# A key-value product in two parts, read in another column order, with half of its fold right behind it

## The chip, the core and the metric

The kernel runs on one core of a Trainium2 chip. A core has a matrix engine (TensorE, "PE" in the profile; its weight loads are listed apart as "PEld"), a vector engine (VectorE, DVE), a scalar engine for activation functions and copies (ScalarE, ACT), a general engine (GpSimd, POOL) and a queue engine that issues most transfers (SyncE, SP). TensorE writes its products to PSUM, an accumulation memory; VectorE and ScalarE read them from there. The main on-chip memory is SBUF, with 128 partitions.

The metric is the device time of one execution in microseconds. The kernel before took 261.73 us (median of three runs, 260.96 to 261.99).

## The reference: two blocks and a gate

x has 2048 tokens of width 640. Block A is linear attention with 32 heads of 20 features; block B is a mixer with an MLP; a gate per token mixes them.

```python
qkv = x @ wqkv                       # q, k, v: 32 heads of 20
phi = lambda t: where(t > 0, t + 1, exp(t)) + 1e-6
pq, pk = phi(q), phi(k)
kv = einsum("bhsd,bhse->bhde", pk, v)          # one 20 x 20 block per head
z = einsum("bhsd->bhd", pk)
o = einsum("bhqd,bhde->bhqe", pq, kv) / (einsum("bhqd,bhd->bhq", pq, z)[..., None] + 1e-6)
a = o @ wo

h = gelu(layernorm(x) @ w1)          # then four quarters of h shifted by +1, -1, +2, -2 tokens
x1 = x + shifted(h) @ w2
b = x1 + gelu(layernorm(x1) @ w3) @ w4          # w3: 640 x 1728
out = g * a + (1 - g) * b            # g = sigmoid((x * gate_w).sum(-1))
```

## The kernel before, in words

The work is written out in a fixed order: each engine runs its instructions in the order of the program text, and semaphores hold an instruction until its inputs and buffers are ready. Tokens are cut into 16 chunks of 128 (four tiles of 512); widths of 640 into 5 chunks of 128.

Block A is rearranged so that v is never computed. First pk = phi(x wk) is made for all tokens (L191 and after), then pq = phi(x wq), transposed (q_unit, L242). `g_unit` (L340) forms G = pk^T x, 640 by 640 and summed over all tokens, along with z. It takes the 640 features of pk in five sets j, each of every fifth feature, so that set j holds features m*5 + j for m = 0 to 127. Each set is copied by ScalarE and turned by a transposing transfer into `gT[:, :, j * 128 : (j + 1) * 128]`. So gT, for each of the 5 chunks of x's width, has 640 columns, ordered by set j and then by m; four consecutive m belong to one head (4 times 5 is 20 features).

The kv product (`kv_unit`, L423) multiplies gT with wv, head by head in effect: groups of 3 heads (60 columns), two of them side by side on two halves of the array, six such group pairs (`NG = 6`; the last has a single group of 2 heads and 40 columns). For each it accumulates over 5 chunks: 55 matmuls. wv is the stationary operand, with 64 or 40 columns; gT is streamed. The result holds all cross products of three heads; a mask (`bmask`) keeps the blocks in which both heads agree. VectorE applies it while it copies from PSUM into `kvT` (L428 for five groups, L432 for the last).

The fold multiplies kvT with wo, `m_mm` (L441), so that attention becomes pq M with M = kv wo; ScalarE evicts each fold group (`m_evac`, L447), M goes through memory outside the core (`m_store`, L450, `m_load`), and the attention products use it much later (L539). The denominator needs u = sum of z times pq, in float32 (`den_add`, L261, on VectorE; u lies over part of xT). It is split into two bfloat16 parts so that TensorE can sum it exactly enough: `den_hi` casts u in two halves of the tokens on ScalarE (L264), `den_lo` takes the difference on VectorE (L267), and `den_mm` sums both over the features of a head (L272).

Block B runs around it. `w1_unit` (L395) multiplies the normalised tokens by w1 for one tile of 512 tokens and column blocks of 128; ScalarE evicts with GELU into hsT at shifted places (L402). Column block 4 holds the rest of the four quarters; its GELU goes into `hx` (L405) and VectorE copies four strips of it to shifted places (L408). Then w2 (L508), layer norm, w3 (L558), attention (L539), w4 (L597, L633) follow, tile by tile.

Every product takes its PSUM buffer from `pair()`, which hands out four buffers of two banks in turn. A product therefore waits until the product four calls earlier has been evicted. At the place of the change the order of calls before is: w1 of tile 0 in three units, the two casts of u, kv, den_lo, layer norm of two chunks of the last tile, w1 of tile 1 for column blocks 0, 1 and 4, the fold of groups 0 to 2, w1 of tile 1 for blocks 2 and 3, the fold of groups 3 to 5 and the denominator.

Of the kernel before, what the change touches and what calls it, by code (L numbers as in the profile page):

```python
# [8 lines left out]
ALU = mybir.AluOpType  # L9
BF16 = mybir.dt.bfloat16  # L10
F32 = mybir.dt.float32
# [5 lines left out]
def kernel(  # L17
# [13 lines left out]
    nc = tc.nc  # L31
    P = 128
    S, D = A_x.shape[1], A_x.shape[2]
    F = B_w3.shape[1]
    H, Dh = 32, 20
    NCH = S // P
    TS = 512
    NT = S // TS
    CPT = TS // P
    DC = D // P  # L40
# [5 lines left out]
    shifts = [1, -1, 2, -2]  # L46
    YMAX = 60.0
    GH = 3
    GW = GH * Dh
    NG = 6  # L50
    HP = P // 2
# [7 lines left out]
    const = ctx.enter_context(tc.tile_pool(name="const", bufs=1))  # L59
# [8 lines left out]
    def pair():  # L68
        return ps.tile([P, 2, 512], F32, name="pp")
# [3 lines left out]
    hsT = const.tile([P, DC, S + 4], BF16)  # L73
# [7 lines left out]
    kvT = const.tile([P, NG, HP], BF16)  # L81
# [10 lines left out]
    hmask = const.tile([P, H], F32)  # L92
    z = const.tile([P, DC], F32)
    hm_bf = const.tile([P, H], BF16)
    bmask2 = const.tile([P, 2, GH * 4], F32)
    bmask = const.tile([P, GH * 4], F32)
    ylog = const.tile([P, NCH], F32)
    gate = const.tile([P, NCH], F32)
    omg = const.tile([P, NCH], F32)
# [12 lines left out]
    gT = wk_sb  # L112
# [35 lines left out]
    for g in (0, 2):  # L148
# [8 lines left out]
                            base=0, pattern=[[-1, P]], channel_multiplier=1)  # L157
    for c in range(0, NCH, CPT):
# [3 lines left out]
                            base=0, pattern=[[-4, H]], channel_multiplier=1)  # L162
    nc.gpsimd.affine_select(out=hmask[:], in_=hmask[:], compare_op=ALU.is_ge, fill=0.0,
                            base=3, pattern=[[4, H]], channel_multiplier=-1)
    nc.gpsimd.tensor_copy(hm_bf[:], hmask[:])
    nc.gpsimd.memset(bmask2[:], 1.0)
    nc.gpsimd.affine_select(out=bmask2[:], in_=bmask2[:], compare_op=ALU.is_ge, fill=0.0,
                            base=0, pattern=[[-HP, 2], [-Dh, GH], [0, 4]], channel_multiplier=1)
    nc.gpsimd.affine_select(out=bmask2[:], in_=bmask2[:], compare_op=ALU.is_ge, fill=0.0,
                            base=Dh - 1, pattern=[[HP, 2], [Dh, GH], [0, 4]], channel_multiplier=-1)  # L170
    nc.gpsimd.tensor_tensor(bmask[:], bmask2[:, 0, :], bmask2[:, 1, :], op=ALU.add)
    nc.gpsimd.memset(kvT[:], 0.0)
    for dc in range(DC):
# [58 lines left out]
    for c in range(2, NCH):  # L232
        pt = pair()
# [19 lines left out]
    halves = (slice(0, S // 2), slice(S // 2, S))  # L253
# [9 lines left out]
    def den_hi(sl):  # L263
        nc.scalar.copy(xT[:, 4, sl], u[:, sl])  # L264
# [57 lines left out]
    def ln1_apply(c, eng=nc.vector):  # L322
        t, cc = divmod(c, CPT)
        if cc == 0:
            lnxT[t] = lnx_p.tile([P, DC, TS], BF16, name="lnxT")
        lnx = work.tile([P, D], BF16, name="ln")
        if eng is nc.scalar:
            nc.scalar.activation(lnx[:], x_sb[:, c, 0:D], ACT.Identity, bias=nmr1[:, c:c + 1], scale=rstd1[:, c:c + 1])
        else:
            nc.vector.tensor_scalar(lnx[:], x_sb[:, c, 0:D], mv1[:, c, 0:1], rstd1[:, c:c + 1],  # L330
                                    op0=ALU.subtract, op1=ALU.mult)
        nc.sync.dma_start_transpose(lnxT[t][:, :, cc * P:(cc + 1) * P], lnx[:])
# [57 lines left out]
    def w1_mm(t, fcs):  # L390
        pt = pair()
        for i, fc in enumerate(fcs):
            for dc in range(DC):
                w = w1_sb[:, dc, CG * fc:CG * fc + P] if fc < 4 else w1x[:, dc, :]
                nc.tensor.matmul(pt[:, i, :], lhsT=w, rhs=lnxT[t][:, dc, :], start=(dc == 0), stop=(dc == DC - 1))  # L395
        return pt

    def w1_evac(t, fcs, pt):
        for i, fc in enumerate(fcs):
            if fc < 4:  # L400
                o = 2 + shifts[fc] + t * TS
                nc.scalar.activation(hsT[:, fc, o:o + TS], pt[:, i, :], ACT.Gelu_apprx_tanh)  # L402
            else:
                hx = hx_p.tile([P, TS], BF16, name="hx")
                nc.scalar.activation(hx[:], pt[:, i, :], ACT.Gelu_apprx_tanh)  # L405
                for g in range(4):
                    o = 2 + shifts[g] + t * TS
                    nc.vector.tensor_copy(hsT[32 * g:32 * (g + 1), 4, o:o + TS], hx[32 * g:32 * (g + 1), :])  # L408

    def w1_unit(t, fcs):  # L410
        w1_evac(t, fcs, w1_mm(t, fcs))

    w1_split = ((0, 1), (2, 3), (4,))

    def kv_unit():
        pt = pair()
        for g in range(NG):
            for fc in range(DC):
                for v in range(2 if g < NG - 1 else 1):
                    q = 2 * g + v  # L420
                    h0, h1 = GH * q, min(GH * (q + 1), H)
                    c1 = min(GW * q + HP, D)
                    nc.tensor.matmul(pt[HP * v:HP * v + c1 - GW * q, 0, g * GW:g * GW + (h1 - h0) * Dh],  # L423
                                     lhsT=wv_sb[:, fc, GW * q:c1],
                                     rhs=gT[:, fc, 0:D].rearrange("p (j h i) -> p j h i", j=DC, h=H)[:, :, h0:h1, :],
                                     start=(fc == 0), stop=(fc == DC - 1))
        n = NG - 1
        nc.vector.tensor_tensor(  # L428
            kvT[:, 0:n, 0:GW].rearrange("p g (r j) -> p g j r", j=DC),
            pt[:, 0, 0:n * GW].rearrange("p (g j r) -> p g j r", g=n, j=DC),  # L430
            bmask[:].unsqueeze(1).unsqueeze(1).broadcast_to([P, n, DC, 4 * GH]), op=ALU.mult)
        nc.vector.tensor_tensor(  # L432
            kvT[0:2 * Dh, n, 0:2 * Dh].rearrange("p (r j) -> p j r", j=DC),
            pt[0:2 * Dh, 0, n * GW:n * GW + 2 * Dh].rearrange("p (j r) -> p j r", j=DC),
            bmask[0:2 * Dh, 0:8].unsqueeze(1).broadcast_to([2 * Dh, DC, 8]), op=ALU.mult)

    def m_mm(g, pt, b0=0):
        for v in range(2 if g < NG - 1 else 1):
            k = GW if g < NG - 1 else 2 * Dh
            for hf in range(2):  # L440
                nc.tensor.matmul(pt[HP * hf:HP * (hf + 1), b0 + v, 0:HD], lhsT=kvT[HP * v:HP * v + k, g, :],  # L441
                                 rhs=wo_sb[HP * v:HP * v + k, g, hf * HD:(hf + 1) * HD], start=True, stop=True)

    def m_evac(g, pt, b0=0):
        n = 2 if g < NG - 1 else 1
        dst = mst4[:, g] if g < 4 else mst2[:, g - 4]
        nc.scalar.copy(dst[:, 0:n, :], pt[:, b0:b0 + n, 0:HD])  # L447
# [6 lines left out]
    def m_load():  # L454
        nc.sync.dma_start(m_sb[:], m_dram[0:D, :].rearrange("(r j) e -> r j e", j=DC))

    for fcs in w1_split:
        w1_unit(0, fcs)
    for sl in halves:
        den_hi(sl)  # L460
    kv_unit()
    for sl in halves:
        den_lo(sl)
    for cc in range(2, CPT):
# [1 line left out]
    ln1_rstd(3, 2, CPT)  # L466
    for cc in range(2):
        ln1_apply(3 * CPT + cc)
    for fc in (0, 1, 4):
        w1_unit(1, (fc,))  # L470
    mps = [pair() for _ in range(3)]
    for g in range(3):
        m_mm(g, mps[g])
    for g in range(3):
        m_evac(g, mps[g])
    for fc in (2, 3):
        w1_unit(1, (fc,))
    mps += [pair() for _ in range(2)]
    for g in range(3, 5):
# [256 lines left out]
```

## Time and profile before

| what | value |
|---|---|
| median of three runs | 261.73 us |
| the profiled execution | 261.98 us, span 260.3 us |
| TensorE busy | 253.8 us, 98% of the span |
| VectorE, ScalarE, GpSimd busy | 147.7, 108.0, 32.4 us |
| kv matmuls (L423) | 55, from 76.86 us |
| fold matmuls (L441) | 12 from 81.23 us, 10 from 84.23 us |
| mask into kvT (L428, L432) | 1030 ns and 356 ns on VectorE |
| casts of u (L264) | two, 1.98 us together, on ScalarE |
| granted TensorE clock | 0.999 of full speed |

The span runs from the first to the last instruction; the execution's time is 1.7 us more. In rows of the profile the first numbers are counts, busy time and the mean duration of one instruction in ns, or, in timelines, the start from the span's beginning and the length. Matmuls overlap in a pipeline, so the mean duration of one is longer than the distance from one to the next.

### The profile page before, as it was taken

What the parts mean: (1) busy time and instruction counts of PE and PEld (TensorE: products, weight loads), DVE (VectorE), ACT (ScalarE), POOL (GpSimd) and SP (SyncE); (2) the same over time, 40 slices, a digit from 0 to 9 for tenths busy, and PEclk for the clock granted to TensorE, in tenths of its full rate; (3) what the DMA queues carried; (4) which work ended last, traced back from release to release, by engine and by line L of the source; (5) the groups of instructions that cost most, each with busy time, mean ns of one, the idle gap of its engine ahead of it and who ended that gap; (6) DMA issues with size and microseconds to landing.
All of it is one profiled execution on the core that took longest, in us unless ns stands there. A gap on an engine that the chain in (4) does not pass through costs nothing.

```text
span 260.3 us, 4189 instructions
## 1 busy us (share of the span) xinstructions
PE 253.8 (98%) x1625; PEld 149.6 (57%) x1648; DVE 147.7 (57%) x272; ACT 108.0 (42%) x168; POOL 32.4 (12%) x86
## 2 busy tenths in 40 slices
PE   6999999999999999999999999999999999999995
PEld 3677555688854644565464566455565546465543
DVE  2488778799999988498300398600287610125132
ACT  3455444465788546432343323342322344342100
POOL 4000040023410340032000131000022000000000
PEclk9999999999999999999999999999999999999999
DMA  8999999016672797964022124213123412211011
GB/s 186 193 139 329 368 272 336 36 29 125 123 103 55 102 154 198 270 199 94 4 40 40 20 53 96 76 24 60 20 52 72 101 23 40 42 48 54 22 51 52
DMA packets 57358, 27.98 MB, mean 108 GB/s; under 512 B 45394, under 2 KB 56442, under 8 KB 57338
## 3 DMA queue, kind: packets, MB, share of 16 engines
q1 hardware_dynamic: 56896, 27.22, 44.8%
q10 hardware_dynamic: 442, 0.49, 0.6%
q8 instruction: 13, 0.21, 0.4%
q14 instruction: 7, 0.06, 0.1%
HBM read 12.86 MB, written 3.47 MB: 63 GB/s over the span
## 4 chain that ended last, share of the span: by engine, by line
PE 96%; DMA 2%; issue 1%; SPq 0%; ACT 0%; DVE 0%
PE pp L558 21%; PE pp L597 16%; PE pp L508 8%; PE pp L340 8%; PE pp L539 8%; PE pp L395 8%; PE pp L242 8%; PE pp L191 8%; PE pp L633 5%; DMA wk_sb<-in_A_wqkv_dram 2%; PE pp L568 1%; PE pp L589 1%; PE pp L423 0%; SPq L122 0%; PE pp L649 0%
## 5 line engine op out<-in xcount | busy, mean ns | idle before, releaser
L558 PE MATMUL pp<-lnxT,w_sb 128*128 128x512 bf16 x249 | 59.8, 379 | 0.6
L560 ACT ACTIVATE h<-pp 128x1024 bf16<-128x1024 f32 (+1 forms) x28 | 27.0, 963 | 56.1 <-PE pp L558 56.1
L597 PE MATMUL pp<-h,w_sb 128*128 128x512 bf16 (+1 forms) x228 | 42.4, 343 | 0.3
L558 PEld LDWEIGHTS <-w_sb 128*128 128x128 bf16 x260 | 25.0, 98 | 27.0 <-issue 0.3
L511 DVE TENSOR_TENSOR x<-pp,x_sb 128x640 f32<-128x640 f32 x16 | 13.1, 816 | 40.1 <-PE pp L508 40.0
L597 PEld LDWEIGHTS <-w_sb 128*128 128x128 bf16 x234 | 22.6, 98 | 19.6 <-issue 1.0
L183 ACT ACTIVATE e<-pp 128x640 bf16<-128x640 f32 (+1 forms) x26 | 21.5, 828 | 9.5 <-PE pp L242 9.4
L303 POOL TENSOR_SCALAR rstd<-mv 128x1 f32<-128x1 f32 (+2 forms) x22 | 9.1, 416 | 127.9 <-DVE mv L309 126.9
L539 PE MATMUL pp<-m_sb,pqT 128*128 128x320 bf16 x160 | 24.3, 299 | 0.0
L545 DVE SCALAR_TENSOR_TENSOR x<-pp,gate,x 128x640 f32<-128x640 f32 x16 | 14.1, 883 | 17.9 <-PE pp L539 12.6
L508 PE MATMUL pp<-w_sb,hsT 128*128 128x320 bf16 x160 | 23.9, 300 | 0.0
L191 PE MATMUL pp<-wk_sb,xT 128*128 128x320 bf16 (+1 forms) x160 | 22.1, 300 | 1.2 <-DMA wk_sb<-in_A_wqkv_dram 1.2
L340 PE MATMUL pp<-x_sb,pk 128*128 128x320 bf16 (+1 forms) x160 | 22.0, 300 | 0.0
L242 PE MATMUL pp<-xT,hsT 128*128 128x512 bf16 x98 | 21.6, 379 | 0.1
L340 PEld LDWEIGHTS <-pk 128*128 128x128 bf16 x160 | 18.8, 117 | 3.2
L508 PEld LDWEIGHTS <-hsT 128*128 128x128 bf16 x160 | 15.5, 98 | 8.4 <-issue 0.4
L610 DVE SCALAR_TENSOR_TENSOR oc<-pqT,omg,x 128x640 bf16<-128x640 bf16 x12 | 10.5, 877 | 17.0 <-DMA pqT<-hx 17.0
L539 PEld LDWEIGHTS <-pqT 128*128 128x128 bf16 x160 | 15.6, 98 | 7.7
L191 PEld LDWEIGHTS <-xT 128*128 128x128 bf16 x160 | 15.6, 98 | 7.5 <-issue 1.4
L395 PE MATMUL pp<-lnxT,w_sb 128*128 128x512 bf16 x77 | 17.9, 379 | 0.3 <-ACT hx L405 0.2
L242 PEld LDWEIGHTS <-hsT 128*128 128x128 bf16 x100 | 11.7, 117 | 9.7
L304 POOL TENSOR_TENSOR rstd<-rstd,mhalf 128x1 f32<-128x1 f32 (+2 forms) x22 | 17.1, 777 | 1.8
(93 smaller groups left out, 248.1 us busy)
## 6 DMA issues: line engine op xcount, KB each, us to landing
x_sb<-in_A_x_dram SPq DMA_DIRECT2D x1, 2240.0 KB
out_dram<-oc SPq DMA_DIRECT2D x14, 160.0 KB, 2.0
w_sb<-in_B_w_dram SPq DMA_DIRECT2D x1, 2160.0 KB, 16.4
w_sb<-in_B_w_dram SPq DMA_DIRECT2D x1, 2080.0 KB, 10.5
hsT<-in_A_wqkv_dram SPq DMA_DIRECT2D x1, 800.0 KB, 5.3
m_sb<-in_A_wqkv_dram SPq DMA_DIRECT2D x1, 800.0 KB, 12.6
w_sb<-in_B_w_dram SPq DMA_DIRECT2D x1, 800.0 KB, 11.6
m_sb<-m_dram SPq DMA_DIRECT2D x1, 800.0 KB, 4.3
```

The costliest lines, as they stand in the source:

```text
L183: nc.scalar.activation(ev, src, ACT.Exp)
L191: nc.tensor.matmul(pt[:, hf, 0:n], lhsT=xT[:, dc, c * P:(c + 1) * P], rhs=wk_sb[:, dc, hf * HD:hf * HD + n], start=(dc == first), stop=(dc ...
L242: nc.tensor.matmul(pt[:, t % 2, :], lhsT=wq_sb[:, dc, :].rearrange("p (m j) -> p j m", j=DC)[:, j], rhs=xT[:, dc, t * TS:(t + 1) * TS], st ...
L304: nc.gpsimd.tensor_tensor(out_ap, out_ap, mhalf[:, 0:out_ap.shape[1]], op=ALU.pow)
L340: nc.tensor.matmul(pt[:, hf, 0:HD + hf], lhsT=w, rhs=x_sb[:, c, hf * HD:(hf + 1) * HD + hf], start=(c == 0), stop=(c == NCH - 1))
L395: nc.tensor.matmul(pt[:, i, :], lhsT=w, rhs=lnxT[t][:, dc, :], start=(dc == 0), stop=(dc == DC - 1))
L508: nc.tensor.matmul(pt[:, hf, 0:HD], lhsT=hsT[:, fc, 2 + c * P:2 + (c + 1) * P], rhs=w2_sb[:, fc, hf * HD:(hf + 1) * HD], start=(fc == 0), ...
L539: nc.tensor.matmul(pt[:, hf, 0:HD], lhsT=pqT[:, j, c * P:(c + 1) * P], rhs=m_sb[:, j, hf * HD:(hf + 1) * HD], start=(j == 0), stop=(j == D ...
L545: nc.vector.scalar_tensor_tensor(x1, pt[:, :, 0:HD], gate[:, c:c + 1], x1, op0=ALU.mult, op1=ALU.add)
L558: nc.tensor.matmul(pt[:, k, :], lhsT=w3_sb[:, dc, fc * P:(fc + 1) * P], rhs=lnT[:, dc, :], start=(dc == 0), stop=(dc == DC - 1))
L560: nc.scalar.activation(h2[:, 2 * i * TS:(2 * i + n) * TS], pt[:].rearrange("p h e -> p (h e)")[:, 0:n * TS], ACT.Gelu_apprx_tanh)
L597: nc.tensor.matmul(dst, lhsT=w4_sb[:, fc, d * P:(d + 1) * P], rhs=st[t]["h2"][:, fc * TS + a:fc * TS + b], start=False, stop=(fc == FF - 1))
```

## The change

The kv product is done in two parts, each with a PSUM buffer of its own: groups 0 to 2 (30 matmuls) and groups 3 to 5 (25). The fold of groups 0 to 2 follows directly, ahead of w1 of tile 1, and its three evictions stand ahead of the four copies of hx and of tile 1's GELUs in the text; w1 of tile 1 then runs without interruption.

The streamed operand of a kv matmul is the same 60 columns of gT in another order. Before, they are read set by set: for each of five j, 12 adjacent columns. Now they are read by m and then j: each column is 128 elements (256 bytes) from the one before. The PSUM columns thereby come out by head and feature in natural order, and the mask writes kvT contiguously, where it wrote every fifth element before. The mask tile grows from 12 to 60 columns, since it no longer repeats over j, and is applied in three instructions: 180 columns, 120 columns and the last group's 40.

The casts of u are split: the first half is cast between the GELUs of column blocks 0, 1 and those of 2, 3 of tile 0, the second after the GELU into hx. The copies of hx are split from the GELU, into a function of their own, and for tile 0 run after the masks.

```diff
-    bmask2 = const.tile([P, 2, GH * 4], F32)
-    bmask = const.tile([P, GH * 4], F32)
+    bmask2 = const.tile([P, 2, GW], F32)
+    bmask = const.tile([P, GW], F32)
...
-                            base=0, pattern=[[-HP, 2], [-Dh, GH], [0, 4]], channel_multiplier=1)
+                            base=0, pattern=[[-HP, 2], [-Dh, GH], [0, Dh]], channel_multiplier=1)
...
-    def w1_evac(t, fcs, pt):
+    def w1_gelu(t, fcs, pt):
...
-                for g in range(4):
-                    o = 2 + shifts[g] + t * TS
-                    nc.vector.tensor_copy(hsT[32 * g:32 * (g + 1), 4, o:o + TS], hx[32 * g:32 * (g + 1), :])
+                return hx
+
+    def w1_shift(t, hx):
+        for g in range(4):
+            o = 2 + shifts[g] + t * TS
+            nc.vector.tensor_copy(hsT[32 * g:32 * (g + 1), 4, o:o + TS], hx[32 * g:32 * (g + 1), :])
...
-    def kv_unit():
+    def kv_mm(g0, g1):
         pt = pair()
-        for g in range(NG):
+        for g in range(g0, g1):
             for fc in range(DC):
                 for v in range(2 if g < NG - 1 else 1):
                     q = 2 * g + v
                     h0, h1 = GH * q, min(GH * (q + 1), H)
-                    c1 = min(GW * q + HP, D)
-                    nc.tensor.matmul(pt[HP * v:HP * v + c1 - GW * q, 0, g * GW:g * GW + (h1 - h0) * Dh],
+                    c1, o = min(GW * q + HP, D), (g - g0) * GW
+                    nc.tensor.matmul(pt[HP * v:HP * v + c1 - GW * q, 0, o:o + (h1 - h0) * Dh],
                                      lhsT=wv_sb[:, fc, GW * q:c1],
-                                     rhs=gT[:, fc, 0:D].rearrange("p (j h i) -> p j h i", j=DC, h=H)[:, :, h0:h1, :],
+                                     rhs=gT[:, fc, 0:D].rearrange("p (j m) -> p m j", j=DC)[:, 4 * h0:4 * h1, :],
                                      start=(fc == 0), stop=(fc == DC - 1))
...
+    def kv_mask(g0, g1, pt):
+        n, k = min(g1, NG - 1) - g0, 2 * Dh
+        nc.vector.tensor_tensor(kvT[:, g0:g0 + n, 0:GW], pt[:, 0, 0:n * GW].rearrange("p (g c) -> p g c", g=n),
+                                bmask[:].unsqueeze(1).broadcast_to([P, n, GW]), op=ALU.mult)
+        if g1 == NG:
+            nc.vector.tensor_tensor(kvT[0:k, NG - 1, 0:k], pt[0:k, 0, n * GW:n * GW + k], bmask[0:k, 0:k], op=ALU.mult)
...
-    for fcs in w1_split:
-        w1_unit(0, fcs)
-    for sl in halves:
-        den_hi(sl)
-    kv_unit()
+    w1_unit(0, w1_split[0])
+    den_hi(halves[0])
+    w1_unit(0, w1_split[1])
+    hx0 = w1_gelu(0, w1_split[2], w1_mm(0, w1_split[2]))
+    den_hi(halves[1])
+    kv_ps = [kv_mm(0, 3), kv_mm(3, NG)]
+    for i in range(2):
+        kv_mask(3 * i, 3 * i + 3, kv_ps[i])
+    mps = [pair() for _ in range(3)]
+    for g in range(3):
+        m_mm(g, mps[g])
+    for g in range(3):
+        m_evac(g, mps[g])
+    w1_shift(0, hx0)
     for sl in halves:
         den_lo(sl)
...
-    for fc in (0, 1, 4):
-        w1_unit(1, (fc,))
-    mps = [pair() for _ in range(3)]
-    for g in range(3):
-        m_mm(g, mps[g])
-    for g in range(3):
-        m_evac(g, mps[g])
-    for fc in (2, 3):
+    for fc in (0, 1, 4, 2, 3):
         w1_unit(1, (fc,))
```

More of the change, by code (lines that the diff above doesn't have):

```diff
@@ L167 @@
     nc.gpsimd.affine_select(out=bmask2[:], in_=bmask2[:], compare_op=ALU.is_ge, fill=0.0,
-                            base=0, pattern=[[-HP, 2], [-Dh, GH], [0, 4]], channel_multiplier=1)
+                            base=0, pattern=[[-HP, 2], [-Dh, GH], [0, Dh]], channel_multiplier=1)
     nc.gpsimd.affine_select(out=bmask2[:], in_=bmask2[:], compare_op=ALU.is_ge, fill=0.0,
-                            base=Dh - 1, pattern=[[HP, 2], [Dh, GH], [0, 4]], channel_multiplier=-1)
+                            base=Dh - 1, pattern=[[HP, 2], [Dh, GH], [0, Dh]], channel_multiplier=-1)
     nc.gpsimd.tensor_tensor(bmask[:], bmask2[:, 0, :], bmask2[:, 1, :], op=ALU.add)
@@ L405, in w1_evac @@
                 nc.scalar.activation(hx[:], pt[:, i, :], ACT.Gelu_apprx_tanh)
-                for g in range(4):
-                    o = 2 + shifts[g] + t * TS
-                    nc.vector.tensor_copy(hsT[32 * g:32 * (g + 1), 4, o:o + TS], hx[32 * g:32 * (g + 1), :])
+                return hx
[3 more added lines that the diff above has]
+            nc.vector.tensor_copy(hsT[32 * g:32 * (g + 1), 4, o:o + TS], hx[32 * g:32 * (g + 1), :])
     def w1_unit(t, fcs):
-        w1_evac(t, fcs, w1_mm(t, fcs))
+        hx = w1_gelu(t, fcs, w1_mm(t, fcs))
+        if hx is not None:
+            w1_shift(t, hx)
     w1_split = ((0, 1), (2, 3), (4,))
-    def kv_unit():
+    def kv_mm(g0, g1):
         pt = pair()
-        for g in range(NG):
+        for g in range(g0, g1):
             for fc in range(DC):
@@ L421, in kv_unit @@
                     h0, h1 = GH * q, min(GH * (q + 1), H)
-                    c1 = min(GW * q + HP, D)
-                    nc.tensor.matmul(pt[HP * v:HP * v + c1 - GW * q, 0, g * GW:g * GW + (h1 - h0) * Dh],
+                    c1, o = min(GW * q + HP, D), (g - g0) * GW
+                    nc.tensor.matmul(pt[HP * v:HP * v + c1 - GW * q, 0, o:o + (h1 - h0) * Dh],
                                      lhsT=wv_sb[:, fc, GW * q:c1],
-                                     rhs=gT[:, fc, 0:D].rearrange("p (j h i) -> p j h i", j=DC, h=H)[:, :, h0:h1, :],
+                                     rhs=gT[:, fc, 0:D].rearrange("p (j m) -> p m j", j=DC)[:, 4 * h0:4 * h1, :],
                                      start=(fc == 0), stop=(fc == DC - 1))
[L427 to L435, printed above, removed]
+        return pt
+    def kv_mask(g0, g1, pt):
[4 more added lines that the diff above has]
+            nc.vector.tensor_tensor(kvT[0:k, NG - 1, 0:k], pt[0:k, 0, n * GW:n * GW + k], bmask[0:k, 0:k], op=ALU.mult)
     def m_mm(g, pt, b0=0):
```

## The prediction

> **What bounds the kernel now.** I read the page's engine totals and its chain of waits first: they say which engine sets the end.
>
> ```profile
> PE 253.8 (98%) x1625; PEld 149.6 (57%) x1648; DVE 147.7 (57%) x272; ACT 108.0 (42%) x168; POOL 32.4 (12%) x86
> ...
> PE 96%; DMA 2%; issue 1%; SPq 0%; ACT 0%; DVE 0%
> ```
>
> TensorE is busy for 98% of 260.3 us and is 96% of the chain. Whatever moves on VectorE or ScalarE counts only through a wait of TensorE; a matmul that gets slower counts in full. Next, the chain in order of time, from 70 to 92 us, which holds everything that the change touches.
>
> ```profile
> 71.81 5.13 PE pp L395 x23
> 76.93 1.02 PE pp L423 x55
> ...
> 81.34 0.61 ACT hx L405
> ...
> 81.99 2.32 PE pp L395 x10
> ...
> 85.38 5.54 PE pp L508 x40
> ```
>
> The 55 kv matmuls (L423) take about 1.0 us; the only other engine on the chain is ScalarE, for which TensorE waits just before 81.99. Third, the timelines of this stretch (start, length, then the row), TensorE's and then VectorE's and ScalarE's.
>
> ```profile
> 75.69 1.24 PE L395 MATMUL pp<-lnxT,w1x 128*128 128x512 bf16 x5
> 76.86 1.09 PE L423 MATMUL pp<-wk_sb,m_sb 128*64 128x60 bf16 x55
> 77.89 2.33 PE L395 MATMUL pp<-lnxT,w_sb 128*128 128x512 bf16 x9
> 80.06 1.24 PE L395 MATMUL pp<-lnxT,w1x 128*128 128x512 bf16 x5
> 81.23 0.60 PE L441 MATMUL pp<-wo_sb,kvT 60*64 60x320 bf16 x12
> 81.99 2.32 PE L395 MATMUL pp<-lnxT,w_sb 128*128 128x512 bf16 x10 [0.15 <-ACT hx L405]
> 84.23 0.60 PE L441 MATMUL pp<-wo_sb,kvT 60*64 60x320 bf16 x10
> 84.76 0.61 PE L272 MATMUL pp<-xT,hm_bf 128*32 128x512 bf16 x8
> ```
>
> ```profile
> 76.53 0.76 DVE L330 TENSOR_SCALAR ln<-x_sb,mv,rstd 128x640 bf16<-128x640 bf16 x2
> 77.60 1.19 DVE L408 COPY hsT<-hx 32x512 bf16<-32x512 bf16 x4 [0.30 <-ACT hx L405]
> ```
>
> ```profile
> 75.89 1.08 ACT L402 ACTIVATE hsT<-pp 128x512 bf16<-128x512 f32 x2 [0.90 <-PE pp L395]
> ```
>
> Three things are to be seen. The twelve fold matmuls at 81.23 need 0.76 us to the next row, the ten at 84.23 (as many groups of four) 0.53: the difference of 0.23 us is the wait for ScalarE. Full-width matmuls of 512 columns come every 0.216 us (ten in 2.16), so the five from 75.69 would end their turn at 76.77, and the kv product starts at 76.86: entering a narrow layout of the array costs 0.09 us. And VectorE is free from 77.29.
>
> The last view is the groups by form: the prices.
>
> ```profile
> L423 PE MATMUL pp<-wk_sb,m_sb 128*64 128x60 bf16 x50 | 1.0, 195 | 0.0
> ...
> L242 PEld LDWEIGHTS <-hsT 128*128 128x128 bf16 x100 | 11.7, 117 | 9.7
> ...
> L508 PEld LDWEIGHTS <-hsT 128*128 128x128 bf16 x160 | 15.5, 98 | 8.4 <-issue 0.4
> ...
> L428 DVE TENSOR_TENSOR kvT<-pp,bmask 128x300 bf16<-128x300 f32 x1 | 1.0, 1030 | 0.0
> ...
> L432 DVE TENSOR_TENSOR kvT<-pp,bmask 40x40 bf16<-40x40 f32 x1 | 0.4, 356 | 0.0
> ...
> L616 DVE SCALAR_TENSOR_TENSOR oc<-pp,omg,x 128x512 bf16<-128x512 f32 x4 | 3.0, 746 | 3.3 <-PE pp L633 3.3
> ...
> L616 DVE SCALAR_TENSOR_TENSOR oc<-pp,omg,x 128x128 bf16<-128x128 f32 x4 | 1.4, 348 | 8.0 <-PE pp L649 7.6 <-PE pp L633 0.4
> ```
>
> **The change, part by part.** TensorE issues the same instructions as before: 55 kv, 22 fold, 50 w1 matmuls and 8 for the denominator. Only their order, their waits and one read pattern differ.
>
> *Removed: the ScalarE wait.* Before, w1's column block 2 of the second token tile takes the PSUM buffer of block 4, whose GELU ends at 81.94. After, the fold stands before these units and block 2's buffer is that of the third fold group, evicted long before. That gains 0.23 us. What is late next? The three evictions start when the fold's first group is done, about 78.6, at 0.6 us apart (three in 1.88); they free buffers at about 79.3, 79.9 and 80.5, and w1 asks for them at about 79.9, 81.0 and 82.1. Nothing waits.
>
> *Moved: the fold of groups 0 to 2 behind kv.* Kv and fold are both narrow, so one change of layout goes: 0.09 us gained.
>
> *Added: the wait for the first mask.* Part 1 is 30 of 55 matmuls; at the present pace (1.0 us for 55) its last one ends near 77.5. The mask on 180 columns follows. Its price by the L616 rows: (746 - 348) / 384 = 1.04 ns a column and 0.22 us fixed, so 0.40 us; by the strided L428 and L432 rows (2.6 ns a column, 0.25 us fixed) 0.72. I take 0.40, because the output is contiguous now. With about 0.05 us for each semaphore (GELU end 81.94 to matmul 81.99) the fold may start at 78.0, and part 2 ends its turn at 77.89. So 0.1 us of waiting, which part 2 covers fully once the kv matmuls are about 0.25 us slower in all (part 2 is 25 of 55 of that); by the dearer price it is 0.4 us at the present pace. Queued behind the mask on VectorE are the second mask, the 40-column one, the four copies of hx and den_lo; all ran later before, and hx is now not waited for.
>
> *Added: the second PSUM buffer.* W1's first unit takes the buffer of part 2, so it waits for masks 2 and 3: 0.04 + 0.12 (120 columns) + 0.26 to 0.36 + 0.05, about 0.5 us after part 2, against 0.43 us for the twelve fold matmuls and the change of layout. Cost 0 to 0.15; I take 0.1.
>
> *Moved: the casts of u.* The first goes between two pairs of GELUs. ScalarE idles 0.90 us there, before 75.89, and half a cast pair is 0.94 from start to start (1.98 for two): it ends its turn within 0.05 us of that. U's first half is ready in time: VectorE writes the last term from 72.11, two halves in 2.48. So nothing, or at most that 0.05 on the GELUs, which delays the second fold group only if it passes 78. The second cast keeps its place, 77.5 to 78.5, and is done when the first fold eviction asks.
>
> *Hidden, at nothing:* the larger masks on GpSimd (L167 and its neighbours at 2.4 to 3.5 us, 70 us ahead); w1_shift, needed only by w2 at 85.4; no DMA is added or moved past another.
>
> *The read pattern: the term that decides.* Before, a kv matmul streams its 60 columns of gT in five runs of 12 adjacent values. After, each column lies 256 bytes from the last, and no two neighbours are adjacent. No row streams an operand like that. The 55 matmuls run in pairs on two halves of the array, so their streams are 25 pairs of 60 columns and 5 single ones of 40: 1,700 columns. At 512 columns in 0.213 us that is 0.71 us of the 1.0. Lower bound: no cost, because runs of 12 already stream at nearly the pace of one run (at 113.66 in the chain twenty 64-column matmuls of L568 take 0.58 us, 29 ns each; a pair here takes about 31). Nearest row on this engine: weights read at a step of 10 bytes cost 117 instead of 98 ns for 128 columns, 0.15 ns a column, 0.25 us for 1,700. Upper row, on another engine: VectorE writes at a step of 10 bytes at 2.6 instead of 1.04 ns a column, 2.5 times; here 1.5 x 0.71 = 1.06 us. A step of 256 bytes is farther than either, so I take the middle to upper part of 0 to 1.06: 0.6 us.
>
> The Trainium skill, "SBUF — State Buffer", Specifications, speaks against the change at this point: memory lines are 16 bytes and full rate needs at least two hits on each. The old runs of 24 bytes meet it, the new order has one hit per line. It gives no price; if one hit in place of two halves the rate (my estimate from that page), the term is 0.71 us and the time 262.2. The L242 row is in line with a cost above nothing, at a milder step.
>
> **Sum.** 0.6 (read) + 0.1 (second buffer) + 0 (mask, covered by slower part 2) - 0.23 (ScalarE wait) - 0.09 (layout) = +0.38 us. Everything later hangs on TensorE's own order (waits of about 0.05), so it reaches the end whole. The profiled execution took 261.98 (span 260.3 and 1.7 around it), which gives 262.36; the median of the three runs is 261.73, 0.25 lower, so 262.1.
>
> **Rivals.**
> 1. *The scattered read is free or nearly so* (0 to 0.25 us). Then 0.1 for the mask's wait stands against the gains: -0.23 - 0.09 + 0.1 + 0.1 = -0.12, up to +0.1: 261.6. For it: runs of 12 cost nothing visible. Against: both strided rows above cost.
> 2. *Slower: the two concurrent streams and their weight loads contend for scattered reads,* four times the present column time instead of about two. Place: the two kv parts alone. Price 3 x 0.71 = 2.1 us; less 0.23 and 0.09, plus 0.1: +1.9, 263.6. It decides from a read cost of 1.5 us (1.3 us is 0.5%), a pair at about 85 ns instead of 31. For it: both halves of the array read the same columns of gT at once, and VectorE's 2.5 is with a step of only 10 bytes. Against: no row shows TensorE's streams disturbing each other; pairs now run at almost the price of one.
> 3. *ScalarE becomes late:* the cast between the GELUs or the evictions ahead of the second tile's GELUs push a PSUM buffer past its user. The nearest margin is 0.05 us at 75.89. With a whole cast late (0.94 us), hx's GELU ends at 78.5, the second cast at 79.4 and the first eviction at 80.1, where w1 asks for its buffer at 79.9: 0.2 us more than the forecast, 262.3; with the evictions 0.6 us later still, 262.9.
> 4. *Clearly faster.* All waiting of TensorE in the stretch is under 0.4 us, so I know no mechanism that gains 1.3.
>
> **How the numbers follow.** 0.5% is 1.3 us, about what a measurement of this kernel can tell from no change. Forecast 0.50 (read cost 0.25 to 1.06: 261.75 to 262.6), rival 1 0.21, rival 2 0.20, rival 3 0.06 (all of it below the 0.5%), rival 4 0.03. Same: 0.50 + 0.21 + 0.06 = 0.77; slower 0.20, faster 0.03. The range reaches from 261.2 (rival 1, with 0.3 for the spread of the runs, 260.96 to 261.99) to 263.7 (rival 2).
>
> **What would show it.** In the profile after: kv's two rows, together about 1.6 us where one had 1.0 (the read cost; 1.0 or 3.1 would show rivals 1 or 2); the fold row directly behind them, with no idle time or 0.1 us for the mask; the mask at 0.40 and not 0.72; w1's first row of the second tile with about 0.1 us behind a mask; no wait for hx; second-tile w2 work starting about 0.4 us later than 85.31. I am wrong if the kv rows are far from 1.6, or if a wait over 0.3 us stands between 76 and 85.

## The result, and the profile after

The changed kernel takes 262.76 us (median of ten runs, 262.37 to 263.24); the kernel before took 261.51 us in ten runs beside it (260.69 to 262.17). The ratio is 1.0049, with a 95% interval of 1.0034 to 1.0065: 1.25 us slower, just inside the 0.5% that was called no change; the interval reaches to both sides of it.

TensorE stays the engine that sets the end. This is the chain of waits of the changed kernel between 68 and 94 us (start, length, row).

```profile
71.33 5.13 PE pp L395 x23
76.45 3.08 PE pp L428 x53
79.53 0.53 PE pp L445 x12
...
80.45 5.13 PE pp L395 x23
85.58 0.53 PE pp L445 x10
86.10 0.55 PE pp L272 x8
86.65 5.54 PE pp L514 x40
```

ScalarE has left the chain: nothing stands between w1's units of the second tile. In its place the kv matmuls (now L428) have grown from about 1.0 us to 3.1. TensorE's timeline of the changed kernel shows the same without gaps:

```profile
75.21 1.24 PE L395 MATMUL pp<-lnxT,w1x 128*128 128x512 bf16 x5
76.39 3.15 PE L428 MATMUL pp<-wk_sb,m_sb 128*64 128x60 bf16 x55
79.46 0.60 PE L445 MATMUL pp<-wo_sb,kvT 60*64 60x320 bf16 x12
80.01 2.33 PE L395 MATMUL pp<-lnxT,w_sb 128*128 128x512 bf16 x9
...
85.51 0.60 PE L445 MATMUL pp<-wo_sb,kvT 60*64 60x320 bf16 x10
86.03 0.62 PE L272 MATMUL pp<-xT,hm_bf 128*32 128x512 bf16 x8
86.58 1.67 PE L514 MATMUL pp<-w_sb,hsT 128*128 128x320 bf16 x11
```

From the first kv matmul to the next kind of work it was 77.89 - 76.86 = 1.03 us and is 79.46 - 76.39 = 3.07. The masks, the first cast of u, GELUs and the fold's evictions, from VectorE's and ScalarE's timelines of the changed kernel:

```profile
78.18 0.35 DVE L436 TENSOR_TENSOR kvT<-pp,bmask 128x180 bf16<-128x180 f32 x1 [1.34 <-PE pp L428]
79.57 0.28 DVE L436 TENSOR_TENSOR kvT<-pp,bmask 128x120 bf16<-128x120 f32 x1 [1.05 <-PE pp L428]
79.77 0.18 DVE L439 TENSOR_TENSOR kvT<-pp,bmask 40x40 bf16<-40x40 f32 x1
```

```profile
74.41 1.03 ACT L264 CAST xT<-xT 128x1024 bf16<-128x1024 f32 x1
75.41 1.08 ACT L402 ACTIVATE hsT<-pp 128x512 bf16<-128x512 f32 x2
...
79.84 1.88 ACT L451 CAST oc<-pp 128x640 bf16<-128x640 f32 x3 [1.82 <-PE pp L445]
```

The mask on 180 columns ends at 78.53, nearly a microsecond before the fold starts. The GELUs at 75.41 follow the first cast without waiting for TensorE.

One measure is used below: the stretch from the first kv matmul to the first w2 matmul, which holds all that differs on TensorE. (Behind it, from the first w2 matmul to the end of the span, the profiles of the kernel before, the changed kernel and the five variants of them that were timed take 174.9 to 175.0 us alike.) It was 85.31 - 76.86 = 8.45 us and is 86.58 - 76.39 = 10.19, so 1.74 more. The spans differ by only 1.2 us, because the profiled execution of the kernel before reached the kv product 0.47 us later: its first large product waited for an input transfer until 6.74 us. TensorE's instructions ahead of kv are the same in all kernels here, and yet kv starts between 75.64 and 76.92 us in them. That spread is in the totals too, and the stretch is free of it.

### The profile page after: what moved, and what is told of

It reads as the page before. It is cut to its first block, busy times and chain, and to the rows that moved or that the text cites. A ratio compares the mean times of both kernels' runs of the same rounds, so it can differ in the third digit from the quotient of the medians.

```text
span 261.5 us, 4190 instructions
## 1 busy us (share of the span) xinstructions
PE 256.6 (98%) x1625; PEld 152.3 (58%) x1648; DVE 147.6 (56%) x273; ACT 108.2 (41%) x168; POOL 32.4 (12%) x86
## 4 chain that ended last, share of the span: by engine, by line
PE 97%; DMA 1%; issue 1%; SPq 0%; DVE 0%
PE pp L564 21%; PE pp L603 16%; PE pp L191 9%; PE pp L514 8%; PE pp L340 8%; PE pp L545 8%; PE pp L395 8%; PE pp L242 8%; PE pp L639 5%; DMA x_sb<-in_A_x_dram 1%; PE pp L428 1%; PE pp L574 1%; PE pp L595 1%; PE pp L445 0%; PE pp L217 0%
## 5 line engine op out<-in xcount | busy, mean ns | idle before, releaser
L191 PE MATMUL pp<-wk_sb,xT 128*128 128x320 bf16 (+1 forms) x160 | 22.7, 305 | 0.0
```

What stands on the lines that cost most here:

```text
L191: nc.tensor.matmul(pt[:, hf, 0:n], lhsT=xT[:, dc, c * P:(c + 1) * P], rhs=wk_sb[:, dc, hf * HD:hf * HD + n], start=(dc == first), stop=(dc ...
```

## The experiments

### The read order taken back, all else kept

```diff
...
-                                     rhs=gT[:, fc, 0:D].rearrange("p (j m) -> p m j", j=DC)[:, 4 * h0:4 * h1, :],
+                                     rhs=gT[:, fc, 0:D].rearrange("p (j h i) -> p j h i", j=DC, h=H)[:, :, h0:h1, :],
...
-        nc.vector.tensor_tensor(kvT[:, g0:g0 + n, 0:GW], pt[:, 0, 0:n * GW].rearrange("p (g c) -> p g c", g=n),
-                                bmask[:].unsqueeze(1).broadcast_to([P, n, GW]), op=ALU.mult)
+        nc.vector.tensor_tensor(
+            kvT[:, g0:g0 + n, 0:GW].rearrange("p g (r j) -> p g j r", j=DC),
+            pt[:, 0, 0:n * GW].rearrange("p (g j r) -> p g j r", g=n, j=DC),
+            bmask[:].unsqueeze(1).unsqueeze(1).broadcast_to([P, n, DC, 4 * GH]), op=ALU.mult)
...
```

> The changed kernel with gT read as before (five runs of 12 adjacent columns) and the mask written with a step again; two parts, fold behind, split casts stay. Theory A (the step of the read is the whole loss): the two kv rows fall from 3.15 us to about 1.1, the first mask takes about 0.7 instead of 0.35 us and holds the fold back by 0.4 us, and the time is 261.3 to 261.9, the same as before. Rival (the split, the early fold or the cast order costs): the time stays near 262.7 though the kv rows are short.

Measured: 261.35 us against 261.32, ratio 1.0002 (0.9971 to 1.0034). TensorE's timeline:

```profile
76.46 1.09 PE L428 MATMUL pp<-wk_sb,m_sb 128*64 128x60 bf16 x55
77.89 0.60 PE L450 MATMUL pp<-wo_sb,kvT 60*64 60x320 bf16 x12 [0.34 <-DVE kvT L436]
78.43 2.33 PE L395 MATMUL pp<-lnxT,w_sb 128*128 128x512 bf16 x9
```

The kv row is back at 1.09 us, and the fold waits 0.34 us for the strided mask (0.4 expected). The stretch is 85.00 - 76.46 = 8.54 us, 0.09 more than before. So the split, the early fold and the split casts are not the loss: what they gain (0.3 us), the mask's wait takes back. The loss of the change is in the read order.

### The read order alone, in the kernel before

```diff
...
-                                     rhs=gT[:, fc, 0:D].rearrange("p (j h i) -> p j h i", j=DC, h=H)[:, :, h0:h1, :],
+                                     rhs=gT[:, fc, 0:D].rearrange("p (j m) -> p m j", j=DC)[:, 4 * h0:4 * h1, :],
...
+        nc.vector.tensor_tensor(kvT[:, 0:n, 0:GW], pt[:, 0, 0:n * GW].rearrange("p (g c) -> p g c", g=n),
+                                bmask[:].unsqueeze(1).broadcast_to([P, n, GW]), op=ALU.mult)
...
```

> The kernel before with nothing but the new read order and the contiguous mask; one kv product at its old place. Theory A: the kv row grows from 1.09 to about 3.15 us and nothing hides it: +2.06 us, about 263.5, slower than the changed kernel, because the gains of its order (about 0.3 us) are missing. Rival B (splitting into two PSUM buffers makes the read slow): the kv row stays near 1.1 and the time at 261.3.

Measured: 263.14 us against 261.32 (263.5 expected), ratio 1.0063 (1.0040 to 1.0086), so 1.05 to 2.25 us slower. TensorE's timeline:

```profile
75.75 3.15 PE L423 MATMUL pp<-wk_sb,m_sb 128*64 128x60 bf16 x55
78.83 2.33 PE L395 MATMUL pp<-lnxT,w_sb 128*128 128x512 bf16 x9
...
82.17 0.60 PE L436 MATMUL pp<-wo_sb,kvT 60*64 60x320 bf16 x12
82.93 2.32 PE L395 MATMUL pp<-lnxT,w_sb 128*128 128x512 bf16 x10 [0.15 <-ACT hx L405]
```

One undivided product, and again 3.15 us. The stretch is 86.25 - 75.75 = 10.50 us: 2.05 more than before, and 0.31 more than the changed kernel, which does not have the wait for ScalarE that stands here in the last line, nor the extra change of layout.

### What a scattered column costs

Two kernels put the same eleven blocks of ten extra matmuls behind the kv product of the kernel before, in opposite orders. Each matmul streams 240 columns of one row of xT; only the order of the columns differs.

```diff
+    row = xT[:, 2, :]
+    sp_ps = pair()
+    N = 240
+
+    def steps(n, step):
+        return row[:, 0:n * step].rearrange("p (n k) -> p n k", k=step)
+
+    out1 = sp_ps[:, 0, 0:N]
+    for _ in range(10):
+        nc.tensor.matmul(out1, lhsT=ident[:], rhs=row[:, 0:N], start=True, stop=True)
...
+    for _ in range(10):
+        nc.tensor.matmul(out1, lhsT=ident[:], rhs=steps(N, 8)[:, :, 0], start=True, stop=True)
+    for _ in range(10):
+        nc.tensor.matmul(out1, lhsT=ident[:],
+                         rhs=row[:, 0:5 * 128].rearrange("p (j m) -> p m j", j=5)[:, 0:48, :], start=True, stop=True)
...
```

> The kernel before with eleven blocks of ten extra matmuls behind the kv product, each of 240 columns from one row of xT with full-width weights (the last block with 64 columns of weights); their products are not read. Only the order of the streamed columns differs: one run; runs of 12, of 4, of 2; single columns at a step of 4, 8, 10 and 16 bytes; the new order of gT (five columns 256 bytes apart, then the next m); the same with 272 bytes; the new order with narrow weights. Theory A (a column that shares no short line of memory with its neighbour costs about four columns, whatever the layout): about 102 ns for runs and for steps up to 8 bytes, about 410 ns for a step of 16 bytes and for both far steps. Rival B (two streams at once disturb each other): all blocks near 102 to 200 ns, since these run alone. Rival C (the distance of 256 bytes hits one bank): only the blocks at 256 bytes are slow, 272 and 16 bytes are not.

Each order was run once, in 289.96 and 288.58 us. The timeline of the first order (the step in each line is in the table under it; L490 has 272 bytes, L493 the narrow weights):

```profile
76.67 1.20 PE L471 MATMUL pp<-xT,ident 128*128 128x240 bf16 x10
77.71 1.19 PE L473 MATMUL pp<-xT,ident 128*128 128x240 bf16 x10
78.73 1.19 PE L475 MATMUL pp<-xT,ident 128*128 128x240 bf16 x10
79.76 2.34 PE L477 MATMUL pp<-xT,ident 128*128 128x240 bf16 x10
81.92 1.25 PE L479 MATMUL pp<-xT,ident 128*128 128x240 bf16 x10
83.01 2.29 PE L481 MATMUL pp<-xT,ident 128*128 128x240 bf16 x10
85.12 2.85 PE L483 MATMUL pp<-xT,ident 128*128 128x240 bf16 x10
87.78 4.41 PE L485 MATMUL pp<-xT,ident 128*128 128x240 bf16 x10
92.02 4.24 PE L487 MATMUL pp<-xT,ident 128*128 128x240 bf16 x10
96.09 4.44 PE L490 MATMUL pp<-xT,ident 128*128 128x240 bf16 x10
100.46 4.25 PE L493 MATMUL pp<-xT,ident 128*64 128x240 bf16 x10
104.64 0.61 PE L395 MATMUL pp<-lnxT,w_sb 128*128 128x512 bf16 x1
105.47 2.79 PE L395 MATMUL pp<-lnxT,w_sb 128*128 128x512 bf16 x8 [0.22 <-issue]
108.09 1.24 PE L395 MATMUL pp<-lnxT,w1x 128*128 128x512 bf16 x5
```

A block's distance to the next start, divided by ten, is the pace of one matmul; by 240, the price of a column.

| line | order of the 240 columns | ns per matmul | ns per column |
|---|---|---|---|
| L471 | one run | 104 | 0.43 |
| L473 | runs of 12 | 102 | 0.43 |
| L475 | runs of 4, starts 64 bytes apart | 103 | 0.43 |
| L477 | runs of 2, starts 32 bytes apart | 216 | 0.90 |
| L479 | single, 4 bytes apart | 109 | 0.45 |
| L481 | single, 8 bytes apart | 211 | 0.88 |
| L483 | single, 10 bytes apart | 266 | 1.11 |
| L485 | single, 16 bytes apart | 424 | 1.77 |
| L487 | the new order of gT, 256 bytes apart | 407 | 1.70 |

At a step of up to 4 bytes, and in runs of 4, a column costs no more than in one run (0.43 to 0.45 ns). From there the price follows the number of different 16-byte pieces touched: a step of 8 bytes touches one for every two columns, 10 bytes one for 1.6, 16 bytes one for each, and 2 x 0.88, 1.6 x 1.11 and 1 x 1.77 are all about 1.77 ns. So the runs show a piece of 16 bytes costing about four columns' time, whether one column of it is used or four. Theory A had this price for single columns (about 410 ns), but not for two on a piece: it expected 102 ns for runs of 2 and for a step of 8 bytes, and they take 216 and 211. Inside their blocks the matmuls with 272 bytes follow each other every 426 ns and those with narrow weights every 406, about as slow as with 256, so neither the distance nor the layout is the cause. These matmuls run alone, without a second stream beside them: rival 2's contention of two streams is not needed either. (Each still loads its weights, but those are the same in all blocks of full width.) The kv matmuls of the changed kernel say so too: by their starts in the trace a pair of 60 columns takes 105 ns, 1.74 ns a column for both streams together, and the single ones of 40 columns take 71 ns, 1.77 a column, with no second stream beside them.

The second order began with the far steps, because in the first the granted clock had fallen to half inside the 16-byte block. These are windows of the first order (stretch, its length, busy time of TensorE, weight loads, VectorE, ScalarE and GpSimd, then the granted clock and two columns on transfers):

```profile
85.00:90.00 5.00, 5.00 (x18) 1.85 (x17) 0.00 (x0) 0.00 (x0) 0.00 (x0) 1.00 0.48 50
90.00:95.00 5.00, 5.00 (x14) 1.52 (x13) 0.00 (x0) 0.00 (x0) 0.00 (x0) 0.52 0.00 0
...
105.00:110.00 5.00, 4.65 (x26) 1.94 (x26) 0.00 (x0) 1.83 (x4) 0.00 (x0) 0.77 0.00 0
```

A mean of 0.52 over 5 us is 0.2 us at full clock and the rest at half, so the fall was at 90.2 us; by the same working the 0.77 puts the return at 107.3.

> The eleven blocks of extra matmuls in the opposite order, the far steps first; their products are not read. Theory: each block keeps its pace (about 407 ns for 240 columns at 256 bytes, 424 at 16 bytes, 267, 213, 107, 217, 103 for the rest), now with the far steps at the full granted clock, and the clock falls to half again within some 10 us of the slow blocks' start. Rival: the far blocks' pace came from the halved clock, and at the full clock they are faster; or the clock falls at the same place in time whatever runs there.

The far step with narrow weights, first in line now, keeps 406 ns per matmul inside its block, that with 272 bytes 426, and every block of the table its pace within 3 ns. The windows of that kernel, read as above:

```profile
76.00:80.00 4.00, 4.00 (x62) 1.78 (x56) 3.66 (x9) 2.35 (x3) 0.81 (x1) 1.00 0.48 91
80.00:82.00 2.00, 2.00 (x6) 0.45 (x5) 1.97 (x4) 0.00 (x0) 0.00 (x0) 0.59 0.00 0
82.00:96.00 14.00, 14.00 (x38) 4.66 (x37) 1.75 (x6) 0.00 (x0) 1.10 (x2) 0.50 0.12 23
96.00:98.00 2.00, 2.00 (x11) 1.10 (x10) 0.00 (x0) 0.00 (x0) 0.00 (x0) 0.64 0.00 0
98.00:104.00 6.00, 6.00 (x47) 4.63 (x46) 0.00 (x0) 0.00 (x0) 0.00 (x0) 1.00 0.01 3
```

The 0.59 puts the fall at 80.4 us, the 0.64 the return at 97.4. So the first nine far matmuls, from 76.7 us at 406 ns each, ran at the full clock and the rest at half, at the same pace. The price is not the clock's: what holds this stream up does not slow down with the array. What it is in the chip no run shows beyond the price per piece of 16 bytes.

### Half the dose: runs of two in the changed kernel

```diff
-                                     rhs=gT[:, fc, 0:D].rearrange("p (j m) -> p m j", j=DC)[:, 4 * h0:4 * h1, :],
+                                     rhs=gT[:, fc, 0:D].rearrange("p (j m i) -> p m j i", j=DC, i=2)[:, 2 * h0:2 * h1, :, :],
...
```

> The changed kernel, but gT is read in runs of two adjacent columns (feature pair, then j, then the feature within the pair); the mask undoes the order, one instruction per group. Theory A, with the prices of the extra matmuls (0.90 ns a column in runs of two against 0.43 in runs of four or more): 1,700 columns cost 0.8 us more than in one run, the kv rows together about 1.8 us, a pair of matmuls about 54 ns, the time 261.6 to 262.1. Rival (any read that is not in one run costs the same, or two adjacent columns are enough for the full rate): a pair at 102 or at 31 ns, the time 262.7 or 261.2.

Measured: 261.58 us against 261.27, ratio 1.0016 (1.0002 to 1.0031). Its timeline:

```profile
76.77 1.74 PE L428 MATMUL pp<-wk_sb,m_sb 128*64 128x60 bf16 x55
78.43 0.60 PE L455 MATMUL pp<-wo_sb,kvT 60*64 60x320 bf16 x12
79.15 2.33 PE L395 MATMUL pp<-lnxT,w_sb 128*128 128x512 bf16 x9
```

The kv rows together take 1.74 us (1.8 expected), a pair 55 ns (54 expected), and the stretch is 85.72 - 76.77 = 8.95 us, 0.50 more than before. From the first kv matmul to the fold it is 78.43 - 76.77 = 1.66 us, 0.63 more than before and not 0.8, because a pair read in runs of 12 takes 32 ns, more than 60 times 0.43. Theory A's price holds at half the dose, and two adjacent columns are not enough for the full rate. The time is at the lower edge of the 261.6 to 262.1 expected.

### Two ways to cover the mask

With the read in runs of 12, only the mask's wait of 0.34 us keeps the new order of work from a gain. The first way, on top of that kernel, puts one unit of w1 in between:

```diff
+    w1_unit(1, (0,))
     mps = [pair() for _ in range(3)]
     for g in range(3):
         m_mm(g, mps[g])
...
-    for fc in (0, 1, 4, 2, 3):
+    for fc in (1, 4, 2, 3):
         w1_unit(1, (fc,))
```

> As the first run of this set (read in runs of 12, strided mask in two parts), but with w1's first unit of tile 1 between the kv product and the early fold, so that 1.08 us of matmuls cover the mask. Theory A: no wait for the mask; 0.4 us less than the first run, 261.1 to 261.5, 0.1 to 0.4 us faster than before. Rival: the wait moves to a PSUM buffer or to ScalarE's evictions and the time is that of the first run.

Measured: 261.07 us, ratio 1.0000 (0.9978 to 1.0021). The timeline after the fold:

```profile
78.21 0.60 PE L450 MATMUL pp<-wo_sb,kvT 60*64 60x320 bf16 x12
78.97 1.24 PE L395 MATMUL pp<-lnxT,w_sb 128*128 128x512 bf16 x5 [0.16 <-ACT hsT L402]
```

The mask's wait is gone and the old wait for a GELU is back: the fold takes three buffers of four, so the unit behind it asks for the buffer of the unit ahead of it, whose GELU has not ended. The stretch is 84.44 - 76.00 = 8.44 us, 0.10 less than without the cover and the same as before. The rival was right about where the time went.

The second way, again on top of the kernel with runs of 12, masks group by group:

```diff
+        for g in range(g0, min(g1, NG - 1)):
+            o = (g - g0) * GW
+            nc.vector.tensor_tensor(
+                kvT[:, g, 0:GW].rearrange("p (r j) -> p j r", j=DC),
...
```

> As the run with the read in runs of 12 (two parts, early fold), but the mask is one instruction per group, so the fold's first group waits for 60 columns (about 0.4 us with its fixed part) and not for 180 (0.7 us). Theory: the wait of 0.34 us in front of the fold falls to about 0.1, the stretch from the first kv matmul to the first w2 matmul from 8.54 to about 8.3 us, 0.15 less than in the kernel before; the time about 261.1 to 261.3. Rival: three instructions in a row delay the later groups or the copies of hx as much as they gain, and the stretch stays at 8.5.

TensorE's timeline, and the last mask from VectorE's:

```profile
76.92 1.09 PE L428 MATMUL pp<-wk_sb,m_sb 128*64 128x60 bf16 x55
78.01 0.68 PE L453 MATMUL pp<-wo_sb,kvT 60*64 60x320 bf16 x12
78.81 2.33 PE L395 MATMUL pp<-lnxT,w_sb 128*128 128x512 bf16 x9
```

```profile
78.40 0.35 DVE L444 TENSOR_TENSOR kvT<-pp,bmask 40x40 bf16<-40x40 f32 x1
```

The fold starts 78.01 - 76.92 = 1.09 us after the first kv matmul instead of 1.43, but from there to w1 it is now 78.81 - 78.01 = 0.80 us instead of 0.54. By the starts in the trace the fold's later groups, which wait for their own masks, lose only 0.05 us of that. The other 0.2 us are a wait of w1's first unit: it takes the PSUM buffer of the second kv part, and the last of the six masks (L444), which frees it, ends only at 78.40 + 0.35 = 78.75. (The chain of waits of this kernel leads from that mask to w1, too.) So the wait has moved from the first mask to the last one. (The kernel with runs of two, whose masks are also one per group, loses 0.17 us at the same place.) The stretch is 85.39 - 76.92 = 8.47 us: 0.07 gained, not 0.25; the rival was nearer. The time was 261.82 us against 261.27, ratio 1.0018 (1.0004 to 1.0032), though its stretch and its profiled span (260.3 us) are about those of the kernel before. Where these 0.5 us come from stays open; the start of the run, which varies as told above, was not separated in the timed runs.

No kernel of this set beats the one before by more than the measurement can tell.

## Why the prediction was right, and where it was wrong

The time lies in the range and the change was slower and within 0.5%, as forecast. But the forecast of +0.38 us was a third of the measured 1.25, and of the five terms the largest was badly mis-sized. By the prediction's own sign its main account was wrong: the kv rows were to take about 1.6 us in all, with 3.1 as the mark of rival 2, and they take 3.15. That the change still stayed within 0.5% is luck: 1.25 us lies just under the 1.3 that this comes to, and the stretch itself grew by 1.74.

- *The read pattern, 0.6 us forecast.* Measured 2.04 us (3.07 - 1.03). This is the step that failed: the bounds of 0 to 1.06 us came from runs of 12, which have 4 or more columns in every piece of 16 bytes, and from steps of 10 bytes, where a piece still serves 1.6 columns. VectorE's factor of 2.5 at 10 bytes was close to TensorE's own (1.11 against 0.43 ns, 2.6); carried on to one column a piece it would have been 1.6 times as much, a factor of 4.1. Whether the two engines' factors agree for one reason or by chance, no run shows. The weight loads' 117 instead of 98 ns misled: their 0.15 ns a column is about a fifth of what a stream pays at the same step of 10 bytes (1.11 - 0.43 = 0.68). Why weights show so little was not tried. Rival 2 had the price (2.1 us), for another reason: contention of two streams, while the extra matmuls cost as much a column with one stream alone.
- *The Trainium skill, "SBUF — State Buffer", Specifications,* was right to speak against the change, and its 16-byte lines agree with the table above. The Trainium skill asks there for two or more hits on a line for full bandwidth; for a streamed matmul operand two are not enough here: they cost 0.88 to 0.90 ns a column, and only four reach 0.43 to 0.45. The estimate of 0.71 us that the prediction worked out from it was low for this reason.
- *The ScalarE wait, -0.23, and the change of layout, -0.09.* Both came: the chain after has no ScalarE in it. The read order alone cost a stretch of 10.50 us, and the rest of the change brought that to 10.19, 0.31 less.
- *The mask's wait, 0 under a slower second part.* Right. The mask took 0.35 us contiguous (0.40 forecast); with strided writing and a fast second part it is a wait of 0.34 us, where 0.4 had been forecast at the dearer price.
- *The second buffer, 0.1.* The fold's twelve matmuls and the turn to w1 took 0.55 us, as against 0.53 for the ten later ones before: 0.02. There was nothing to spare: the last mask ends at 79.95 and w1 starts at 80.01. Where the second part is fast and every group has a strided mask of its own, this wait is 0.2 us, as shown above.
- *The casts.* Nothing, as forecast: the GELUs at 75.41 follow the cast directly and hx's at 76.49.

The sum with the measured read cost is 2.04 - 0.23 - 0.09 + 0.02 = 1.74 us, which is the difference of the two stretches. The medians' 1.25 (0.89 to 1.70 by the interval) is less. The spread of the start may be the reason, but that is not shown: the profile after began the stretch 0.47 us earlier, and whether it does so on average was not tried.

## What to carry to other kernels

When an edit turns a contiguous write into a scattered read, ask which engine now pays: here VectorE saved 0.58 us on its masks (1.39 before, 0.81 after), off the chain, and TensorE, which is the chain, paid 2.04 us. For an operand streamed by TensorE, count the columns that share 16 bytes: with four 2-byte values or more it ran at full rate here, with two at half, with one at about a quarter (0.43, 0.90 and 1.77 ns a column). If an order of columns has to be undone, the place is the copy on an engine with time to spare. And when a product is cut into parts, ask two things of the copies behind it: when the first lets the next product start, and when the last gives its buffer back.

## What the runs showed that was not expected

TensorE's clock fell while scattered columns were streamed. In the reversed set of extra matmuls the granted clock fell to half at 80.4 us, 3.6 us after the first far block began at 76.7, and came back at 97.4; in the first order it fell at 90.2, 2.4 us into the 16-byte block, and came back at 107.3. TensorE was listed as busy throughout the scattered blocks. That the slow streams are the reason is inferred from one run of each order: the fall moved with them, and the blocks at full pace before 79.76 us in the first order show none. What sets the moment of the fall is not shown.

Both times the low clock lasted 17.1 us, and in the first order it outlasted the scattered blocks by 2.6 us. The dense matmuls behind them paid for it: the two w1 units from 104.64 to 108.09 us took 3.45 us, where the same ones take 2.17 in the kernel before (77.89 to 80.06). The product in the changed kernel takes 3.15 us at a scattered pace, and the clock stayed at 1.00 there, so this kernel paid only for the stream itself; a longer scattered product would risk its neighbours too.
